# Cutting an output projection in two around other matmuls, and loading the next stage's first inputs early, in a kernel that alternates recurrent attention and gMLP

**Chip, cores, metric.** One core of a Trainium2 chip. The metric is the time of one execution on the device in microseconds (us).

## The reference, cut to what matters

```python
def _A_ref(x, mem0, Wq, Wk, Wv, Wo, seg_len):       # S=2048, D=512, H=32 heads of 128, M=8, seg=32
    mem = mem0
    for s in range(n_seg):                          # 64 segments, one after the other
        h = concat([mem, x[segment s]])             # 8 memory rows + 32 tokens
        q, k, v = h @ Wq, h @ Wk, h @ Wv
        p = softmax(masked(q k^T * scale))
        o = (p v) @ Wo
        mem = o[:, :M]                              # the next segment starts from this
        outs.append(o[:, M:])
def _B_ref(x, w_in, w_sp, b_sp, w_out):             # gMLP
    z = gelu(x @ w_in); z1, z2 = halves(z); z2 = layernorm(z2)
    return (z1 * (w_sp @ z2 + b_sp)) @ w_out
x = x + _A_ref(layernorm(x), ...); x = x + _B_ref(layernorm(x), ...)
x = x + _A_ref(layernorm(x), ...); x = x + _B_ref(layernorm(x), ...)
```

The memory makes attention a chain of 128 segments (64 in each of two blocks). Nothing of segment s+1's memory rows exists before segment s has gone through Wo.

## The kernel before

A segment is one sequence on TensorE. PV is the product of probabilities and values, Wo the output projection; a **change of form** is the switch of TensorE from tiles of one shape (say 128x32) to tiles of another (64x128). The four "fillers" (`fill()`) are matmuls of other work, put where TensorE would wait: projections for the next tile of 128 tokens (`psb`), or an output projection that is not urgent (`pwB`). Of the 64 segments of a block, 45 have `psb` as filler, 12 have `pwB` and 7 have none.

```python
            psS = att.tile([P, 2, 512], F32, name="psS")
            scores(0)                                  # psS: 128x64 tiles; E = exp on ScalarE
            qk_T(3, r3)
            psV = [attO[r].tile([P, 2, 512], F32, name="psV") for r in range(2)]
            v_mm(0, psV[0][:, 0, :])
            fill()                                     # 4 matmuls
            close(0)                                   # mask on VectorE
            nc.vector.tensor_copy(VA[:, 0]..., psV[0][:, 0, :])
            scores(1)
            close(1)
            v_mm(1, psV[1][:, 0, :])
            fill()                                     # 4 matmuls
            nc.scalar.copy(VA[:, 1]..., psV[1][:, 0, :])
            psM = accB.tile([P, 512], F32, name="psM")
            ...                                        # sums for the memory rows: 4 matmuls
            psO = [attO[r].tile([P, 2, 512], F32, name="psO") for r in range(2)]
            pv(0)
            pv(1)                                      # PV of both halves of the heads
            ...                                        # psD: sums for the token rows
            fill()                                     # 8 matmuls
            ...                                        # ScalarE: Rm = 1/psM, Rt = 1/psD by Ln and Exp
            for r in range(2):
                nc.vector.tensor_tensor(out=hview(uT_cur, r, 0, 8), in0=oview(r, 0, 8), in1=...Rm..., op=ALU.mult)
            ...
            spare()                                    # y_add and other work of VectorE
            pw = accB.tile([P, 512], F32, name="pw")
            wo_pass(pw, uT_cur)                        # Wo: 128 weight loads + 128 matmuls
            if s + 1 < NSEG:
                build_hA(s + 1, pw)                    # the next segment's memory rows
            ...
            fill()                                     # 16 matmuls
```

The start of gMLP: w_in whole in two requests, turned row tiles one by one.

```python
        nc.gpsimd.dma_start(w_in_sb[:, :, 0:FH], w_in_v[:, :, FH:FF])
        nc.gpsimd.dma_start(w_in_sb[:, :, FH:FF], w_in_v[:, :, 0:FH])
        ...
        for tt in range(3):
            load_xnT(tt)                               # turning transfer (DMA transpose) of one row tile
        ...
        for tt in range(NT):
            project(tt)
            if tt + 3 < NT:
                load_xnT(tt + 3)
```

The softmax here doesn't subtract the row's maximum and nothing guards it: scores larger than these inputs give would overflow.

## Time and profile before

| | before |
|---|---|
| time, median of 3 runs | 1901.09 us (1898.73 to 1903.06) |
| span of the profiled run | 1906.2 us |
| TensorE busy | 93% |
| segments 0 to 60 of block 0, block 1 | 710.2, 710.5 us |
| segments 61 and 62 together, block 0, block 1 | 33.1, 28.0 us |
| gMLP: projections, block 0, block 1 | 48.2, 47.2 us |
| gMLP: gates and what follows, block 0, block 1 | 125.1, 111.7 us |

The lower part of the table is cut from the trace at the starts of TensorE's groups: a segment begins with its first q matmul (`psm`), the projections with the first `pz`, the gates with the first `pg`; the gates of the last block are counted to TensorE's last matmul. A line of a timeline gives start, duration, engine, source line, operation, output and inputs, and in brackets the idle time just before it with what ended it ("issue": nothing that the profile shows). Durations of matmuls hold latency (a matmul of Wo is recorded with 0.22 us, but 128 of them start within 1.88 us), so what a group costs is the start of the next group minus its own start.

### The profile page before, as it was taken

How to read it: one execution, taken by the hardware profiler on the slowest of the kernel's cores; microseconds unless marked ns; L12 is line 12 of the kernel's file. 1: busy time of each engine (PE TensorE's matmuls, PEld its weight loads, DVE VectorE, ACT ScalarE, POOL GpSimd, SP SyncE). 2: the span in 40 equal slices, each digit the busy share in tenths (PEclk: the TensorE clock that was granted, in tenths of full speed). 3: DMA queues.
4: the chain of work that ended last, by engine and by line, in shares of the span. 5: the costliest groups of instructions: out<-in, count | busy, mean ns of one | idle time of the engine just before them, and what ended most of it. 6: DMA issues, size and time to landing. Idle time of an engine off the chain costs nothing.

```text
span 1906.2 us, 94643 instructions
## 1 busy us (share of the span) xinstructions
PE 1769.2 (93%) x43752; PEld 1020.2 (54%) x43776; DVE 1154.8 (61%) x2700; ACT 1137.9 (60%) x2134; POOL 130.5 (7%) x273
## 2 busy tenths in 40 slices
PE   2999999999999999689989999999999999988898
PEld 1555555555555555335545555555555555544455
DVE  1666666676667766483346666666766676655622
ACT  1666766666666667362136666666766666755511
POOL 5000000000000000022010000000000000002000
PEclk8999999999999999899999999999999999999999
DMA  9100000021002101366640000001200120025554
GB/s 347 43 22 18 18 18 19 22 76 30 18 23 74 29 15 29 97 155 151 141 142 21 21 21 21 21 21 43 79 24 21 51 73 21 15 77 144 115 137 102
DMA packets 165525, 119.93 MB, mean 63 GB/s; under 512 B 112216, under 2 KB 140648, under 8 KB 165128
## 3 DMA queue, kind: packets, MB, share of 16 engines
q1 hardware_dynamic: 143528, 65.11, 13.9%
q0 software_dynamic: 10304, 34.07, 5.7%
q10 hardware_dynamic: 11296, 14.70, 2.6%
q8 instruction: 342, 5.60, 1.2%
q14 instruction: 55, 0.45, 0.1%
HBM read 59.29 MB, written 33.56 MB: 49 GB/s over the span
## 4 chain that ended last, share of the span: by engine, by line
PE 83%; DMA 7%; DVE 4%; issue 3%; ACT 2%; SPq 1%; POOL 0%; DVEq 0%; ACTq 0%; POOLq 0%
PE psm L506 24%; PE psV L506 12%; PE pw L561 12%; PE psb L506 9%; PE pg L306 7%; PE psS L664 5%; PE psO L687 4%; PE pwB L573 3%; PE py L331 2%; PE psD L738 2%; PE pz L245 2%; DMA bsp_bf<-in_B_b_sp_dram 1%; PE psM L728 1%; DMA xs<-xd 1%; DMA xnT<-xb_d 1%
## 5 line engine op out<-in xcount | busy, mean ns | idle before, releaser
L506 PEld LDWEIGHTS <-hA 128*32 128x32 bf16 x12288 | 305.3, 96 | 327.3 <-DVE hA L618 58.9
L643 ACT CAST rows<-psm 128x512 bf16<-128x512 f32 x512 | 299.8, 586 | 203.3 <-PE psm L506 203.3
L561 PE MATMUL pw<-Wo_sb,uT 128*32 128x128 bf16 x16640 | 268.2, 220 | 40.3 <-issue 33.1
L506 PE MATMUL psm<-Wq_sb,hA 128*32 128x512 bf16 x4096 | 279.4, 386 | 22.0 <-DVE hA L618 18.7
L561 PEld LDWEIGHTS <-uT 128*32 128x32 bf16 x16640 | 237.0, 97 | 90.1 <-DVE uT L748 46.1
L506 PE MATMUL psm<-Wk_sb,hA 128*32 128x512 bf16 x4096 | 273.4, 383 | 0.4 <-ACT rowsB L548 0.4
L506 PE MATMUL psV<-Wv_sb,hA 128*32 128x512 bf16 x4096 | 268.0, 382 | 0.0
L647 DVE STREAM_TRANSPOSE QQ<-rows 128x512 bf16<-128x512 bf16 x256 | 182.0, 711 | 90.4 <-ACT rows L643 90.3
L668 ACT ACTIVATE E<-psS 128x448 bf16<-128x448 f32 x256 | 140.0, 547 | 117.8 <-PE psS L664 117.8
L647 DVE STREAM_TRANSPOSE KA<-rows 128x512 bf16<-128x512 bf16 x256 | 181.9, 710 | 40.9 <-ACT rows L643 37.6
L699 DVE TENSOR_TENSOR uT<-psO,Rt 128x384 bf16<-128x384 f32 x256 | 137.9, 539 | 105.4 <-ACT Rt L751 105.4
L748 DVE TENSOR_TENSOR uT<-psO,Rm 128x128 bf16<-128x128 f32 x256 | 62.4, 285 | 180.2 <-PE psD L738 180.2
L306 PE MATMUL pg<-z2n,wspT 128*128 128x344 bf16 x1024 | 161.5, 311 | 0.0
L751 ACT ACTIVATE Rt<-Rt 128x512 f32<-128x512 f32 x256 | 157.4, 629 | 4.1
L611 POOL COPY QQ<-QTB 128x256 bf16<-128x256 bf16 x128 | 51.2, 401 | 1370.3 <-PE psS L664 824.8
L664 PEld LDWEIGHTS <-KA 128*64 128x64 bf16 x2048 | 79.8, 113 | 106.0 <-DVE KA L647 105.2
L746 ACT ACTIVATE Rt<-psD 128x1024 f32<-128x1024 f32 x128 | 131.1, 1024 | 6.1
L506 PEld LDWEIGHTS <-hB 128*32 128x32 bf16 x3072 | 78.4, 96 | 95.7 <-DVE hB L521 26.2
L306 PEld LDWEIGHTS <-wspT 128*128 128x128 bf16 x1024 | 95.7, 98 | 53.0 <-issue 6.8
L671 DVE TENSOR_TENSOR E<-E,maskN 128x448 bf16<-128x448 bf16 x256 | 95.0, 371 | 41.7 <-ACT E L668 41.7
L506 PE MATMUL psb<-Wq_sb,hB 128*32 128x512 bf16 x1024 | 88.6, 385 | 27.3 <-DVE hB L521 27.3
L664 PE MATMUL psS<-QQ,KA 128*64 128x80 bf16 x2048 | 109.9, 208 | 1.1
(127 smaller groups left out, 2300.9 us busy)
## 6 DMA issues: line engine op xcount, KB each, us to landing
Wo_sb<-in_A_Wo_dram POOLq DMA_DIRECT2D x8, 1024.0 KB, 13.5
xs<-xd ACTq DMA_DIRECT2D x32, 256.0 KB
o_d<-o_sb SPq DMA_DIRECT2D x126, 64.0 KB
y_o<-o_d SPq DMA_DIRECT2D x24, 256.0 KB
xd<-y_o SPq DMA_DIRECT2D x22, 256.0 KB
Wq_sb<-in_A_Wq_dram POOLq DMA_DIRECT2D x8, 512.0 KB, 7.3
Wk_sb<-in_A_Wk_dram POOLq DMA_DIRECT2D x8, 512.0 KB, 11.3
Wv_sb<-in_A_Wv_dram POOLq DMA_DIRECT2D x8, 512.0 KB, 11.3
```

The costliest lines, as they stand in the source:

```text
L306: nc.tensor.matmul(pg[t][:, k, 0:344], lhsT=wsp[t][:, st, :], rhs=z2n[:, st, 344 * k:344 * k + 344], start=(st == 0), stop=(st == NT - 1))
L506: nc.tensor.matmul(ps[32 * cg:32 * cg + 32, :], lhsT=lhs(kt, cg), rhs=rhs(kt, cg), start=(kt == 0), stop=(kt == KT - 1), tile_position=(0, ...
L561: nc.tensor.matmul(po[32 * cg:32 * cg + 32, 0:128], lhsT=lhs[:, n, :], rhs=wo_rhs(h, cg), start=(h == 0), stop=(h == H - 1), tile_position ...
L643: nc.scalar.copy(r[:], ps[:])
L647: nc.vector.transpose(out=QQ[:, j % 2, :, 0:32] if j < 2 else KA[:, j % 2], in_=r[:])
L664: nc.tensor.matmul(pS[64 * g:64 * g + 64, i, c0:80 if K is KA else 112], lhsT=K[:, r, n:n + 2, :].rearrange("p h k -> p (h k)"), rhs=q if ...
L668: nc.scalar.activation(out=E[:, r], in_=pS, func=ACT.Exp, scale=scale)
L671: nc.vector.tensor_tensor(out=E[:, r], in0=E[:, r], in1=maskN[:, j4, :].unsqueeze(1).to_broadcast([P, 4, 112]), op=ALU.mult)
L687: nc.tensor.matmul(o if V is VA else ends(o), lhsT=V[64 * g:64 * g + 64, r, i, :], rhs=E[64 * g:64 * g + 64, r, i, c0:c1].rearrange("p (s ...
L699: nc.vector.tensor_tensor(out=hview(uT_nxt, r, 8, 32), in0=oview(r, 8, 32), in1=Rr[:, :, :, 0:24], op=ALU.mult)
L746: nc.scalar.activation(out=Rt[:], in_=psD[:], func=ACT.Ln)
L751: nc.scalar.activation(out=rt, in_=rt, func=ACT.Exp, scale=-1.0)
```

## The change

Its intent: Wo waits for products (`uT`) that wait for the reciprocal of the memory sums, so give TensorE something between. Wo goes in two halves of the heads; the second half's PV and a filler stand between them; the memory sums go per half, so that the first half's come early. For the hand-over to gMLP, w_in comes in four pieces and the first turned row tiles are asked for before attention ends, two row tiles per turning transfer. Three things that go with it are not in the cut: the PSUM buffers of the scores and of the token sums are split by halves, `ln_turn` of the next 128 tokens moves from before Wo to the end of the segment, and the loads of w_sp come two tiles earlier. The diff cut to its core (`...` marks cuts):

```diff
+class _Front:                       # one space: first attention's old buffers, later w_in and turned rows
+    def load_w(self, kt):
+        self.nc.gpsimd.dma_start(self.w_in_sb[:, kt, 0:FH], self.w_in[:, kt, FH:FF])
+        self.nc.gpsimd.dma_start(self.w_in_sb[:, kt, FH:FF], self.w_in[:, kt, 0:FH])
+    def load_rows(self, q):
+        lo = KT * FF + 2 * KT * P * (q % 2)
+        t = self.take(lo, 2 * KT * P).rearrange("p (kt t) -> p kt t", kt=KT)
+        self.nc.sync.dma_start_transpose(out=t, in_=self.xb_d[2 * P * q:2 * P * (q + 1), :]...)
...
-            load_x(t)
+            if t + 2 < NT:
+                load_x(t + 2)                        # residual rows two tiles earlier
...
             scores(1)
             close(1)
-            v_mm(1, psV[1][:, 0, :])
-            fill()
-            nc.scalar.copy(VA[:, 1]..., psV[1][:, 0, :])
-            ...                                      # psM in 4 matmuls
-            pv(0)
-            pv(1)
+            mem_sums(0)                              # 4 small matmuls
+            mem_inverse(0)
+            v_mm(1, psV1[:])
+            nc.scalar.copy(VA[:, 1]..., psV1[:])
+            pv(0)
+            mem_out(0)
+            mem_sums(1)
+            mem_inverse(1)
             ...                                      # psD
             fill()
...
-            wo_pass(pw, uT_cur)
+            wo_pass(pw, uT_cur, range(0, H // 2))
+            pv(1)
+            mem_out(1)
+            fill()
+            ...
+            tok_out(0)
+            wo_pass(pw, uT_cur, range(H // 2, H))
...
             def tail():
+                if tb == NB - 1:                     # the last four segments
+                    front.load_w(j4)
+                    if j4 > 1:
+                        front.load_rows(j4 - 2)
```

## The prediction

> **What bounds the kernel now.** I read the page's first table, then the groups, then the PE timeline of ordinary segments, then the chain and the waits around the two hand-overs from attention to gMLP.
>
> The page's first table, and two groups (busy, mean ns | idle just before, releaser):
>
> ```profile
> PE 1769.2 (93%) x43752; PEld 1020.2 (54%) x43776; DVE 1154.8 (61%) x2700; ACT 1137.9 (60%) x2134; POOL 130.5 (7%) x273
> ...
> L561 PE MATMUL pw<-Wo_sb,uT 128*32 128x128 bf16 x16640 | 268.2, 220 | 40.3 <-issue 33.1
> L561 PEld LDWEIGHTS <-uT 128*32 128x32 bf16 x16640 | 237.0, 97 | 90.1 <-DVE uT L748 46.1
> ```
>
> TensorE is the bound. The trap is the last line: the weight-load row waits 46.1 us for uT before Wo, which is the wait that this change goes after. But the matmul row just above it was idle only 40.3 us before Wo, and 33.1 of that is "issue", not uT: while the weights wait, the filler's matmuls still stream. The PE timeline of one segment (start, duration, group):
>
> ```profile
> 526.02 0.39 PE L506 MATMUL psb<-Wq_sb,hB 128*32 128x512 bf16 x4
> 526.34 0.23 PE L664 MATMUL psS<-QQ,KA 128*64 128x80 bf16 x2
> ...
> 527.91 0.23 PE L728 MATMUL psM<-E,onesG 128*128 128x128 bf16 x1
> ...
> 528.24 0.21 PE L687 MATMUL psO<-E,VA 64*128 64x80 bf16 x2
> ...
> 528.74 0.44 PE L738 MATMUL psD<-E,ones 64*128 64x256 bf16 x8
> 529.11 0.62 PE L506 MATMUL psb<-Wq_sb,hB 128*32 128x512 bf16 x8
> 529.55 1.97 PE L561 MATMUL pw<-Wo_sb,uT 128*32 128x128 bf16 x128
> 531.43 1.05 PE L506 MATMUL psb<-Wk_sb,hB 128*32 128x512 bf16 x16
> ```
>
> Durations contain latency, so I read start to start. The filler psb x8 holds PE 0.44 us (529.11 to 529.55) when Wo follows: both use 128x32 tiles, so 0.22 per four. The filler psb x4 at 526.02 holds it 0.32 when psS follows, in 128x64 tiles. So **a change of tile form costs about 0.10 us** (0.095 at finer resolution; the four psM take 0.33, of which their starts explain 0.23). PV to psD (both 64x128) costs nothing extra. A segment with filler is 11.10 us from first q matmul to the next one if nothing disturbs it, and I find no dependency stall in it. Segments without filler (seven per attention block) take 11.00.
>
> But the segments of the middle of both blocks average about 11.6. The extra is holes like this one inside a group:
>
> ```profile
> 761.38 1.41 PE L561 MATMUL pw<-Wo_sb,uT 128*32 128x128 bf16 x87 [0.36 <-DVE uT L748]
> 766.46 1.33 PE L561 MATMUL pw<-Wo_sb,uT 128*32 128x128 bf16 x41 [3.67 <-issue]
> 773.40 1.90 PE L506 MATMUL psm<-Wq_sb,hA 128*32 128x512 bf16 x16 [5.61 <-DVE hA L618]
> ```
>
> This is the worst (3.67 us); common ones are 0.6 to 1.0 us. They recur at multiples of 256 PE instructions, and the instruction queue of the page has 342 packets of 16 KB: 64 bytes times 256, and 342 times 256 is PE's 87,500 instructions. So PE waits for its program. Wo is 256 instructions in 1.88 us, the densest stretch.
>
> The third line, with the chain around it, shows the hand-over:
>
> ```profile
> 758.29 9.61 DMA o_d<-yB
> 767.91 2.59 DMA y_o<-o_d
> 770.53 0.70 DVE y_o L184
> ```
>
> A store of yB takes 9.6 us because the whole of w_in (1.4 MB) and three turned row tiles were sent at 753; y_add waits for it, and hA stands behind y_add on DVE. Inside gMLP the waits view has this, which delays PE once by 3 us:
>
> ```profile
> DVE xo L340 <- DMA xs<-xd: 31.7, 6, 8.0
> ```
>
> [...] after the 5.61 us wait above, 16 matmuls take 1.68 us start to start, against 0.87 warm.
>
> **The change, part by part.**
>
> 1. *New order on PE.* Before, from psS of half 1: S, V1, filler, M, O0, O1, D, filler, Wo, filler. After: S, M0, V1, O0, M1, D, filler, Wo first half, O1, filler, Wo second half, filler. The four fillers remain, with the same work, but one sits at a later place. Tile forms: S 128x64; V, filler, Wo 128x32; M 128x128; O and D 64x128. In this stretch before: S-V, filler-M, M-O, D-filler, four changes. After: S-M, M-V, V-O, O-M, M-D, D-filler, Wo-O, O-filler, eight. Four more at 0.095 are 0.38 us a segment. The sums per half are eight matmuls of 64 columns for four of 128: about 0.28 us for 0.23, estimated from the 0.035 us pairs of PV; +0.05. PV cut in two: +0.01. Together **+0.44 us**, all on the path, because PE is full there.
>
> 2. *Refill.* A line of 256 instructions that begins with Wo lasts 1.88 us now. After: 128 instructions of Wo in 0.97, 32 of PV in 0.36, 16 of filler in 0.44, 80 of Wo in 0.58, so 2.35 us. A stalled line lasts 2.9 to 3.6 us from its beginning in the trace. The worst hole thus shrinks by about 0.47 us, and averaged over all places where a line's end can fall I get 0.43 going to 0.27: **-0.16 us**. Adding the 8 instructions per segment takes little of it back.
>
> 3. *Sum for attention.* +0.28 us for 114 segments with filler is +32 us. Without filler: the 0.43 wait before Wo goes, but the second half now waits 0.5 for its own product after PV, and there are the drains: +0.2 for 14, +3. Attention: **+35 us**. ScalarE (two Ln of 512 columns for one of 1024, two small Ln and Exp more) and VectorE have 25 to 30% free in a segment and stay out of the way.
>
> 4. *w_in in four pieces over the last four segments, turned rows two segments before the end.* The two segments after seg 60 of each block take 20.27 and 12.81, then 14.50 and 13.47, against 11.00: 17 us lost, counting the half clock. I expect 2 to remain: **-15 us**.
>
> 5. *Two row tiles per turning transfer.* Now a turned tile is asked for when the tile three before is done, and comes up to 5.8 us later (asked 813.9, used 819.7): 1.3 to 1.8 us lost three times per gMLP. With pairs, each is asked two tiles (4.65 us) ahead, so the same loss. The projection takes 48 us where matmuls need 37, but VectorE is busy 39 of the 48 (norms), and the last rows wait for late norms. I book **0**.
>
> 6. *Residual rows loaded two tiles earlier.* The xs waits (3.2 us once, 1.4 twice with slow clock after it) are all in the first gMLP; gone: **-6 us**.
>
> Sum: 1901 + 35 - 15 - 6 = 1915.
>
> **The rivals.** (a) *The wait for uT is real and goes*: 46 us from the weight-load row, so 1901 - 46 - 21 = 1834. For it: that row. Against it: the matmul row's 5.2 us, and the back-to-back starts above. I hardly believe it. (b) *The refill holes vanish altogether*, because the filler in the middle of Wo gives the queue time: 0.43 x 114 = 49 us, against +53 of drains and +0 to 3, minus 21: 1885. For it: Wo is where most holes lie. (c) *A new wait*: the product of half 1 comes only after the second PV, with about 0.5 us of latency against 0.44 us of filler: a tie. VectorE may be held there by y_add. 0.2 us more per segment is 25 us: 1940. (d) *The turned pairs come late*, each wait twice as long, with half clock after it: +8 us, 1923.
>
> **Range and chances.** My sum is 1915. Rival (b) in part is likelier than (c), as the author must have seen some gain, so I say 1909. Attention may be off by 12 us each way, gMLP by 6: 1884 to 1933 holds 8 in 10. Faster by 2% needs 1863, which even (b) does not reach: 0.04. Slower by 2% needs 1939, as in (c): 0.06. The same: 0.90.
>
> **What would show it.** The undisturbed segment grows from 11.10 to about 11.54 us; each of the psM halves, PV halves and both sides of the second PV shows a 0.1 us gap between starts. The weight-load row's wait for uT falls while the time does not. Issue holes before and in Wo fall by about a third. Segments 61 and 62 of each block are near 11.2; xs waits go. The prediction is wrong if drains are hidden (segment under 11.3), if holes vanish, or if Wo's second half waits for uT by more than 0.1 us.

Three of its words stand for measurements. A drain is the 0.10 us that the trace has at a change of form; more than that gap is not shown. The half clock is the granted clock of 0.50 after the wait of 5.61 us (773.40 to 775.08 us) and after one of 3.02 us (903.16 to 906.00). A line of 256 is a packet of the page's instruction queue: 342 of 16 KB before and 346 after, for 87,528 and 88,576 weight loads and matmuls, 256 to each. For the -0.16 us the length of a stalled line is the trace's (segments 2 to 60, from 256 instructions earlier to the end of the stall: 2.4 to 3.6 us, eight in ten 2.8 to 3.4; after, 2.8 to 3.8); the rest of that term is the author's estimate.

## More of the kernel before

TensorE, VectorE and ScalarE run in the order of the text. In the attention block the two engines that issue most DMAs (SyncE, GpSimd) don't: there the framework orders the requests by when it reckons their buffers free.

The profiled run of before took 1908 us by its own clock, 8 us more than the timed median beside the changed kernel (1899.9).

## The result

The changed kernel took 1911.57 us (median of 4 runs, 1910.17 to 1913.9) against 1899.91 for the kernel before, run beside it (4 runs, 1896.72 to 1903.06). The ratio is 1.0063, with a 95% interval of 1.0042 to 1.0083. "The same" by the 2% measure, and slower by 0.6%: 12 us, with 8 to 16 in the interval. The prediction had 8 (1909 for 1901).

The page's first table and the two Wo groups, after:

```profile
PE 1815.1 (95%) x44288; PEld 1044.8 (55%) x44288; DVE 1170.5 (61%) x2700; ACT 1177.4 (62%) x2518; POOL 136.0 (7%) x285
...
L582 PE MATMUL pw<-Wo_sb,uT 128*32 128x128 bf16 x16640 | 285.5, 219 | 19.9 <-issue 10.7
L582 PEld LDWEIGHTS <-uT 128*32 128x32 bf16 x16640 | 244.7, 97 | 90.2 <-DVE uT L745 56.8
```

The weight-load row still waits for uT, now 56.8 us instead of 46.1: that wait was not what the kernel paid for, and it did not go away. What fell is the row above it: idle before Wo from 40.3 to 19.9 us, of that "issue" from 33.1 to 10.7. TensorE is busier (93% to 95%) and not done sooner: the added time is booked as work. The PE timeline of one segment after, from the first half's memory sums to the last filler:

```profile
532.93 0.29 PE L737 MATMUL psM<-E,onesG 128*128 128x64 bf16 x4
533.15 1.05 PE L527 MATMUL psV<-Wv_sb,hA 128*32 128x512 bf16 x16
534.13 0.21 PE L707 MATMUL psO<-E,VA 64*128 64x80 bf16 x2
...
534.70 0.45 PE L774 MATMUL psD<-E,ones 64*128 64x256 bf16 x8
535.08 0.40 PE L527 MATMUL psb<-Wq_sb,hB 128*32 128x512 bf16 x4
535.30 1.07 PE L582 MATMUL pw<-Wo_sb,uT 128*32 128x128 bf16 x64
536.30 0.21 PE L707 MATMUL psO<-E,VA 64*128 64x80 bf16 x2
...
536.64 0.61 PE L527 MATMUL psb<-Wq_sb,hB 128*32 128x512 bf16 x8
537.17 1.08 PE L582 MATMUL pw<-Wo_sb,uT 128*32 128x128 bf16 x64
538.08 1.04 PE L527 MATMUL psb<-Wk_sb,hB 128*32 128x512 bf16 x16
```

Read start to start. psV holds TensorE for 0.98 us (533.15 to 534.13), where it held it for 0.87 before a filler of its own tile form: 0.11 for the change of form. The first half of Wo takes 1.00 (535.30 to 536.30) and the second 0.91: again a change of form. The filler of eight ahead of the second half takes 0.53 (536.64 to 537.17) where eight before Wo took 0.44 before: this 0.08 to 0.09 is a wait for the second half's product, which the timeline of the weight loads names:

```profile
537.17 0.90 PEld L582 LDWEIGHTS <-uT 128*32 128x32 bf16 x64 [0.41 <-DVE uT L745]
```

The shortest segments with filler are now 11.58 us long, before 11.10. Against the groups of a segment of before, the 0.48 are: psV +0.11, the sums +0.11, PV +0.18, psD +0.01, the filler of four -0.09 (its change of form is gone), Wo with the filler behind it +0.08, and +0.08 for the filler ahead of Wo's second half.

Phase by phase from the two traces:

| us | before | after | difference |
|---|---|---|---|
| start | 43.0 | 42.4 | -0.6 |
| segments 0 to 60, both blocks | 1420.6 | 1443.0 | +22.4 |
| segments 61 and 62, both blocks | 61.1 | 45.3 | -15.7 |
| segment 63, Wo, pwB, both blocks | 46.0 | 44.7 | -1.3 |
| gMLP projections, both blocks | 95.4 | 98.5 | +3.1 |
| gMLP gates and next start, both blocks | 236.8 | 232.1 | -4.7 |

I call **hole** what a segment is longer than the shortest segment of its kind (pwB filler, psb filler, none). The mean hole of segments 2 to 60 fell from 0.41 to 0.15 us (mean of the two blocks), and the holes over 0.25 us from 58 to 24 in both blocks.

### The profile page after: what moved, and what is told of

Same layout as the page of the kernel before. It is cut to its first block, busy times and chain, and to the rows that moved or that the text cites. A ratio compares the mean times of both kernels' runs of the same rounds, so it can differ in the third digit from the quotient of the medians.

```text
span 1909.5 us, 96179 instructions
## 1 busy us (share of the span) xinstructions
PE 1815.1 (95%) x44288; PEld 1044.8 (55%) x44288; DVE 1170.5 (61%) x2700; ACT 1177.4 (62%) x2518; POOL 136.0 (7%) x285
## 4 chain that ended last, share of the span: by engine, by line
PE 89%; DVE 4%; DMA 3%; issue 2%; POOL 1%; ACT 1%; DVEq 0%; ACTq 0%; SPq 0%; POOLq 0%
PE psm L527 23%; PE pw L582 13%; PE psV L527 12%; PE psb L527 10%; PE pg L321 8%; PE psS L684 5%; PE psO L707 4%; PE pwB L594 3%; PE psM L737 3%; PE psD L774 2%; PE py L347 2%; PE pz L261 1%; DMA Wo_sb<-in_A_Wo_dram 1%; PE pT L338 1%; DMA Wv_sb<-in_A_Wv_dram 1%
## 5 line engine op out<-in xcount | busy, mean ns | idle before, releaser
L582 PE MATMUL pw<-Wo_sb,uT 128*32 128x128 bf16 x16640 | 285.5, 219 | 19.9 <-issue 10.7
L582 PEld LDWEIGHTS <-uT 128*32 128x32 bf16 x16640 | 244.7, 97 | 90.2 <-DVE uT L745 56.8
L527 PE MATMUL psm<-Wq_sb,hA 128*32 128x512 bf16 x4096 | 272.0, 383 | 10.3 <-DVE hA L638 8.9
L527 PE MATMUL psm<-Wk_sb,hA 128*32 128x512 bf16 x4096 | 268.6, 380 | 0.0
L745 DVE TENSOR_TENSOR uT<-psO,Rm 128x128 bf16<-128x128 f32 x256 | 74.7, 292 | 267.6 <-PE psO L707 263.5
L778 ACT ACTIVATE Rt<-psD 128x512 f32<-128x512 f32 x256 | 136.4, 584 | 0.0
L527 PEld LDWEIGHTS <-hB 128*32 128x32 bf16 x3072 | 73.6, 97 | 83.6 <-DVE hB L542 25.4
L569 ACT CAST rowsB<-psb 128x512 bf16<-128x512 f32 x128 | 74.5, 582 | 56.4 <-PE psb L527 51.0
```

The source lines that it names most:

```text
L527: nc.tensor.matmul(ps[32 * cg:32 * cg + 32, :], lhsT=lhs(kt, cg), rhs=rhs(kt, cg), start=(kt == 0), stop=(kt == KT - 1), tile_position=(0, ...
L582: nc.tensor.matmul(po[32 * cg:32 * cg + 32, 0:128], lhsT=lhs[:, n, :], rhs=wo_rhs(h, cg), start=(h == 0), stop=(h == H - 1), tile_position ...
L778: nc.scalar.activation(out=Rt[:, g, :], in_=psD[g][:], func=ACT.Ln)
```

## The experiments

Twelve kernels ran, each in five rounds against the kernel before, in four sessions. All outputs are right.

**1. The parts apart.** `e1_front_only` has the attention order of before and all the rest of the change; `e2_order_only` has only the new attention order.

```diff
 e1_front_only: the changed kernel, with
-            mem_sums(0) ... wo_pass(pw, uT_cur, range(0, H // 2)); pv(1); fill(); wo_pass(pw, uT_cur, range(H // 2, H))
+            v_mm(1, ...); fill(); psM; pv(0); pv(1); psD; fill(); wo_pass(pw, uT_cur)     # as before
 e2_order_only: the kernel before, with exactly the opposite edit
```

> The attention order of before, with everything else of the change (w_in in pieces, pairs of row tiles per turning transfer, earlier wsp and residual loads). Theory (the terms add): the two segments after number 60 of each block fall from 33.1 and 28.0 us to about 22, gMLP's gate phase loses its residual-row waits, the projection gains 2 us twice: about 19 us less than before, near 1881, and the undisturbed segment stays 11.10 us. Rival (the hand-over gain was luck of the profiled run, which was 8 us longer than the timed ones): only 10 us less, near 1890.

> The new attention order alone, gMLP and its loads as before. Theory (eight changes of tile form instead of four, shorter program waits): 22 to 32 us more than before, 1922 to 1932, undisturbed segment 11.58 us. Rival (the new order is neutral on the clock and the loss of the whole lies in gMLP): 1900. The slow hand-over of before (33.1 and 28.0 us for two segments) should be back.

Measured, against 1903.81 us for before in that session: `e1_front_only` 1891.04 us, ratio 0.9926 (0.9907 to 0.9944); `e2_order_only` 1937.96 us, ratio 1.0172 (1.0150 to 1.0194). So the new order costs about 33 us (22 to 32 expected, with the expected shortest segment of 11.58 us), and the rest gives back about 14. For `e1_front_only` the number is the rival's (1890, expected if the slow hand-over was luck of one profiled run), but the trace is the theory's: the hand-over does fall as expected. The theory missed mainly because it booked a gain of 4 us on the projections. The product of the two ratios is 1.0097; the changed kernel has 1.0063, some 6 us better. In the trace of `e2_order_only` segments 61 and 62 are worse than before (34.2 and 31.4 us in the two blocks), which is 4.5 us of that. In the trace of `e1_front_only` segments 61 and 62 fall to 22.5 and 23.4 us, and the gates by 4.4, but the projections grow by 4.0.

**2. Pairs of row tiles undone.** On `e1_front_only`, one row tile per turning transfer, in four slots, so tile t + 4 is asked for after tile t (three tiles lie between, as the expectation counts it) and as soon as its slot is free:

```diff
-        lo = KT * FF + 2 * KT * P * (q % 2)
-        ...dma_start_transpose(out=t, in_=self.xb_d[2 * P * q:2 * P * (q + 1), :]...)
+        lo = KT * FF + KT * P * (q % 4)
+        ...dma_start_transpose(out=t, in_=self.xb_d[P * q:P * (q + 1), :]...)
...
+            if tt + 4 < NT:
+                front.load_rows(tt + 4)
```

> As e1, but one row tile per turning transfer in four slots, so that each is asked for three tiles ahead instead of two. Theory (a turned pair asked two tiles ahead comes late by about 1.6 us three times per projection): the projection falls from 49 to about 45 us, 4 to 8 us less than e1 in all. Rival (VectorE's norms and the last rows' late norms bound the projection, transfers are hidden anyway): the same as e1 within 2 us.

Measured 1886.31 us, ratio 0.9899 (0.9881 to 0.9918). The same program ran three times more (experiment 6), and the mean of its four ratios is 0.9909, so by the times alone the gain over `e1_front_only` is 0.2%, no more than the scatter. The phase itself is a little clearer: both projections together take 98.3 to 99.9 us in four of the five kernels with pairs (98.5 in the changed kernel, 99.4 in `e1_front_only`, 98.3 in `e4_pv_joined`, 99.9 in `e8_after_shift`) and 94.6 to 96.4 in the seven runs with single tiles. The fifth with pairs, `e9_sums_whole`, takes 95.1, though TensorE idles as long there as in the changed kernel (17.6 and 17.9 us): its last two tiles run at full clock (granted clock 1.00, 4.65 us), where those of the changed kernel get 0.63 and 0.71 (7.3 and 6.5 us). So the phase moves by some 3 us with whether a lower clock follows the last wait, and that the longer projections come from the pairs is likely but not shown. The view of `pz` has what ended the idle time before it, first of the changed kernel, then of `e3_single_tiles`:

```profile
  DMA front<-xb_d: 14.8, 6
  ACT z L264: 3.1, 4
```

```profile
  ACT z L264: 9.5, 6
  DMA front<-xb_d: 7.9, 2
```

Both lines are TensorE's: us, and how often. Six waits for turned rows (14.8 us) became two (7.9), while TensorE waits more often for ScalarE to free `pz` (9.5 for 3.1), so that only part is gained. The two that remain are one in each gMLP, for the last tiles, whose normalised rows are themselves late (in block 0 they are stored from 835.35 us on, and the transfers go out at 837.39). One sees them in the changed kernel too, with a lower clock behind (granted 0.63, 24 matmuls in 7.49 us; elsewhere 4.81, at 1.00):

```profile
842.14 4.81 PE L261 MATMUL pz<-front 128*128 128x512 bf16 x24 [0.68 <-ACT z L264]
852.27 7.49 PE L261 MATMUL pz<-front 128*128 128x512 bf16 x24 [5.32 <-DMA front<-xb_d]
```

This is the best version found: by the mean of its four ratios 0.9% faster than before, and 1.5% faster than the changed kernel.

**3. The second PV joined to the first stretch.** On the changed kernel, `pv(1)` goes right after psD, so two changes of form fall away and only a filler of eight stands between the halves of Wo (not in the cut: psM and the second half of V exchange their PSUM buffers):

```diff
             ...                                      # psD
+            pv(1)
             fill()
+            mem_out(1)
...
             wo_pass(pw, uT_cur, range(0, H // 2))
-            pv(1)
-            mem_out(1)
             fill()
```

> The changed kernel with the second PV moved back from between the Wo halves to straight after the sums of tokens, where it has the same tile form; two changes of form fewer, Wo still in halves with the filler between, memory sums still per half. Theory (a change of form costs 0.095 us of PE each): undisturbed segment 11.39 us instead of 11.58, 20 us less than the changed kernel, near 1891, less up to 6 us if the program waits grow because Wo's halves are now closer. Rival (the second PV between the halves gives the program queue the time it needs): program waits go back to those of before and the time stays near 1905 to 1911. Rival (drains are hidden): segment stays 11.58.

Measured 1902.94 us, ratio 0.9991 (0.9975 to 1.0006). The shortest segment falls from 11.58 to 11.26 us: psD 0.38 to 0.29 and the first half of Wo 1.00 to 0.89 (the two changes of form, 0.20), the filler of eight 0.53 to 0.43 (the wait for the product). Three of the same lines of `e4_pv_joined`:

```profile
543.92 1.07 PE L582 MATMUL pw<-Wo_sb,uT 128*32 128x128 bf16 x64
544.82 0.60 PE L527 MATMUL psb<-Wq_sb,hB 128*32 128x512 bf16 x8
545.25 1.07 PE L582 MATMUL pw<-Wo_sb,uT 128*32 128x128 bf16 x64
```

But the holes grew from 0.15 to 0.35 us per segment. Of the 0.32 us gained in work, 0.20 went back into holes, which leaves 0.12 x 114 = 14 us; by the ratios it is 14 (0.9991 against 1.0063). (The two traces give 10.5 us for segments 0 to 60: with `pwB` filler the shortest segment fell by 0.10 only.) What came back is not all TensorE's program. Of the idle stretches over 0.15 us in segments 2 to 60 of both blocks, those without a releaser went from 7.2 to 19.0 us, but 7.6 us are new waits for ScalarE to empty `psb`, up to 1.44 us at once, of which the changed kernel has none. So PV between the halves costs changes of form and saves waits for the program and for ScalarE; about half of what came back is shown to be the program's.

**4. Where the holes come from.** `e5_shift` is `e3_single_tiles`, `e8_after_shift` the changed kernel, each with 128 more TensorE instructions once at the very start, half of a line of 256:

```diff
+        if first:
+            dmy = accB.tile([P, 512], F32, name="dmy")
+            for k in range(64):
+                nc.tensor.matmul(dmy[:, 0:128], lhsT=ones[:], rhs=ones[:], start=True, stop=True, ...)
         ln_turn(0)
```

> Built on e3: 64 extra 128x128 matmuls (128 TensorE instructions) once at the very start, with an output nobody reads; every later instruction moves by half of a 256-instruction line. Theory (the holes inside segments are waits for TensorE's program, one per line, and cost where a line's end falls together with dense small matmuls): the single holes move to other segments and groups, their sum in each block stays within 4 us of e3's (27 and 24 us), and the time is that of e3 within 0.3% (ratio .987 to .993). Rival (the holes are waits for data or for another engine): they stay in the same segments, within a segment of where they were. Third possibility: e3 has a lucky place of its lines; then the sum moves by over 6 us and the ratio by over 0.4%.

> The changed kernel with the same 128 extra instructions at the start. Theory (the new order needs less queue time than the old one wherever the lines end): holes stay near 0.15 us per segment (before 0.41), time that of the changed kernel within 0.3% (ratio 1.003 to 1.009 over before). Rival (the small holes of the changed kernel are luck of where its lines end): holes go up to 0.3 per segment and the time by 15 us (ratio 1.014).

Lengths of seven segments of block 0 (56 and 52 have pwB filler, at least 11.43; the others at least 11.10), from the starts of their first matmuls:

| segment | 52 | 53 | 54 | 55 | 56 | 57 | 58 |
|---|---|---|---|---|---|---|---|
| before | 11.43 | 11.78 | 11.10 | 12.18 | 11.43 | 11.48 | 11.10 |
| e3_single_tiles | 11.43 | 11.74 | 11.10 | 11.90 | 11.47 | 12.34 | 11.10 |
| e5_shift | 12.44 | 11.10 | 12.08 | 11.10 | 12.15 | 11.10 | 11.35 |

The PE timeline has two of them as breaks within Wo, in `e3_single_tiles`:

```profile
671.60 0.34 PE L582 MATMUL pw<-Wo_sb,uT 128*32 128x128 bf16 x9 [0.45 <-issue]
694.27 0.68 PE L582 MATMUL pw<-Wo_sb,uT 128*32 128x128 bf16 x33 [0.62 <-issue]
```

These are in segments 53 and 55. In `e5_shift` the corresponding ones are in segments 52 and 54:

```profile
662.02 0.34 PE L582 MATMUL pw<-Wo_sb,uT 128*32 128x128 bf16 x9 [0.78 <-issue]
685.21 0.51 PE L582 MATMUL pw<-Wo_sb,uT 128*32 128x128 bf16 x21 [0.80 <-issue]
```

The holes jumped to the segments that had been whole, at the same data and the same work. The table shows where it is clearest: of the 62 holes over 0.25 us of `e3_single_tiles` in both blocks, 31 shrank to under 0.1, and 20 segments still have one over 0.25. The count of instructions settles it. Number TensorE's instructions in each trace in order of time (weight loads, matmuls and its semaphore instructions). In segments 2 to 60 of both blocks TensorE has 54 idle stretches over 0.15 us without a releaser in the kernel before (28.5 us), 16 in the changed kernel (7.2 us), 54 in `e3_single_tiles` (29.8) and 56 in `e5_shift` (36.2). Every one of them stands at the same place of its 256: the number modulo 256 is 194, and in three of the four traces it drops once, for all that follow, by 1 (before: by 13), presumably where records are missing; in the changed kernel it is 194 throughout. And in the traces of before and after each of them (54 and 16) ends 1.2 to 1.6 us after a packet of 16 KB of the instruction queue has landed: TensorE waited for its program. Of the stretches with a named releaser (in before 6.0 us for `hA`, 2.2 for `uT`, 0.4 for a copy of ScalarE) none stands there; those are waits for data, also counted in what I call holes.

The sum of the holes over segments 2 to 60 was 28.3 and 30.1 us in the two blocks, in `e3_single_tiles` 27.2 and 23.6 (23.5 to 24.6 in block 1 in its three repeats, experiment 6). In block 1 that is 6.4 us more, where I had allowed 4 and set over 6, with a ratio over 0.4% off, as the sign of a lucky place. The ratio did not move so far, but where the lines end does matter a little. The time was 1889.13 us, ratio 0.9927 (0.9906 to 0.9948), against 0.9899 to 0.9917 for the unshifted program. `e8_after_shift` took 1911.84 us, ratio 1.0049 (1.0031 to 1.0067), with a mean hole of 0.15 us, the same as without the shift. So the small holes of the new order are no luck of where its lines end.

**5. The memory sums whole again.** On the changed kernel, all four matmuls of the memory sums after the first PV:

```diff
-            mem_sums(0)
-            mem_inverse(0)
             v_mm(1, psV1[:])
             nc.scalar.copy(VA[:, 1]..., psV1[:])
             pv(0)
-            mem_out(0)
-            mem_sums(1)
-            mem_inverse(1)
+            ...                                      # psM as before: 4 matmuls, one Ln, one Exp
+            mem_out(0)
```

> The changed kernel with the memory sums not halved: all four matmuls of them after the first PV. Theory A (the halving only costs: one more change of tile form and eight small matmuls for four, as the prediction counted it): segment 11.58 to 11.43, about 18 us faster than the changed kernel, ratio .997. Theory B (the halves buy time for the first uT: from the sums' end the Ln of 0.38, the Exp of 0.42 and the product of 0.25 us take 1.25 us, and only psD and one filler of four stand between, 0.6 us): the first half of Wo waits 0.5 us for uT in each segment, segment about 11.95; some of it is given back by fewer program holes, so time +30 over the changed kernel, ratio about 1.022.

Measured 1985.66 us, ratio 1.0443 (1.0420 to 1.0465), some 72 us slower than the changed kernel, more than twice what the second theory expected. The PE timeline of a segment of `e9_sums_whole`:

```profile
372.29 0.40 PE L527 MATMUL psb<-Wq_sb,hB 128*32 128x512 bf16 x4
373.23 1.08 PE L582 MATMUL pw<-Wo_sb,uT 128*32 128x128 bf16 x64 [0.54 <-DVE uT L734]
```

The filler of four holds TensorE for 0.94 us instead of 0.23: Wo's first half waits 0.7 us for its product even in the shortest segments. The shortest segment is 12.11 us (11.95 expected). The holes did not shrink in exchange: 0.21 us on average, for 0.15. Here the wait for uT is real, and it shows on the matmul row of the page, not only on the weight-load row:

```profile
L582 PE MATMUL pw<-Wo_sb,uT 128*32 128x128 bf16 x16640 | 283.7, 220 | 95.6 <-DVE uT L734 80.6
L582 PEld LDWEIGHTS <-uT 128*32 128x32 bf16 x16640 | 235.9, 97 | 177.8 <-DVE uT L734 159.6
```

Without the halves of the sums, then, the new order costs another 0.53 us a segment. The prediction counted them only as a cost.

**6. The hand-over: three edits that changed nothing.** On `e3_single_tiles`, I moved the requests for w_in and for the turned rows in the text:

```diff
 e7_w_whole:      -  front.load_w(j4)
                  +  if j4 == 0:
                  +      for k in range(4): front.load_w(k)
 e10_rows_early:  -  if j4 > 1:
                  -      for k in range(2): front.load_rows(2 * (j4 - 2) + k)
                  +  for k in {0: (0, 1, 2), 3: (3,)}.get(j4, ()): front.load_rows(k)
 e11_both_early:  both
```

> Built on e3: all four pieces of w_in are asked for at the end of segment 60, the turned row tiles stay where e3 has them. Theory A (the volume of w_in, 1.4 MB in one go, delayed the store of yB and the reads behind it): segments 61 and 62 go back from 22.5 us towards 33 in block 0 and 28 in block 1, time +10 to +15 over e3, ratio about .997. Theory B (the turning transfers that stood in front of that store in SyncE's queue delayed it): segments 61 and 62 stay under 24 us and the time is e3's, ratio .988 to .992.

> Built on e3: w_in stays in pieces over the last four segments, but the first three turned row tiles are asked for at the end of segment 60, as the kernel before did. Theory B (the turning transfers in SyncE's queue ahead of the store of yB, 1.2 to 2.6 us each on the queue, hold that store and the reads behind it): segments 61 and 62 go back towards 33 us in block 0 and 28 in block 1 from 22.6 and 22.8; time +10 to +15 over e3, ratio about .997. Rival (it takes both, the volume of w_in and the turning transfers at once): segments 61 and 62 stay under 25 us, ratio .988 to .993.

> As e10_rows_early, and all of w_in asked for at the end of segment 60 too: the arrangement of the kernel before. Both theories expect 33 and 28 us for segments 61 and 62 (ratio about .997); it tells whether the volume adds anything to what the turning transfers do alone: theory B says nothing above 2 us, the rival says all of it. If this one stays under 25 us too, the cause lies in neither and is where the kernel before allocates the tiles or issues the requests.

Measured 1886.06, 1890.38 and 1889.07 us, ratios 0.9911 (0.9890 to 0.9931), 0.9917 (0.9900 to 0.9933) and 0.9910 (0.9895 to 0.9925); segments 61 and 62 stayed at 22.4 to 23.3 us. A comparison of the instruction streams showed that on all five engines the three kernels are `e3_single_tiles`, instruction for instruction in the same order: the framework had put the requests where their buffers come free. In `e7_w_whole` and in `e3_single_tiles` alike the pieces of w_in start at 701, 707, 739.5 to 740.3 and 753.7 to 754.5 us. The three say nothing of the cause. They do measure how well one program repeats: 0.9899, 0.9910, 0.9911, 0.9917. A difference of 0.2% between two kernels means nothing here.

**7. The hand-over again, moved by the buffers.** A request can be held back by what its buffer must wait for. In `e12_rows_last`, the first two turned row tiles lie where segment 60's product reads last; in `e13_w_whole_last`, w_in comes in two whole requests that overlap what that product reads.

```diff
 e12_rows_last:    -  lo = KT * FF + KT * P * (q % 4)
                   +  lo = KT * P * (q % 4)                       # w_in moves up by 4 * KT * P
                   -  wo_last(G, range(8 * q, 8 * q + 8), pwB)
                   +  wo_last(G, range(8 * (3 - q), 8 * (3 - q) + 8), pwB)
 e13_w_whole_last: -  dma_start(self.w_in_sb[:, kt, 0:FH], self.w_in[:, kt, FH:FF])    # and the other half
                   +  if kt == 0: dma_start(self.w_in_sb[:, :, 0:FH], self.w_in[:, :, FH:FF])    # and the other half
```

> e7, e10 and e11 turned out to be e3's program instruction for instruction on the DMA queues (the framework orders SyncE and GpSimd by when the buffers are free, not by the place in the text), so they tested nothing of the hand-over. Here the buffers do it: on e3, the first two turned row tiles lie where segment 60's product reads last, so the turning transfers can only start after it, ahead of the store of yB; the pieces of w_in come earlier still. In the kernel before that store was issued 3.4 us later than in e3 (758.3, after two turning transfers) and landed 9.6 us after its issue instead of 4.1. Theory 1 (queue order): segment 61 of block 0 grows by about 3.4 us or more, to 14 or more. Theory 2 (volume alone): stays at 11.2 to 11.4. Time over e3 +0 to +7 us, ratio .990 to .994.

> On e3, w_in in two whole requests as in the kernel before, which can only start after segment 60's product; the turned row tiles stay early as in e3. Theory 2 (volume): the store of yB takes about 5.5 us longer to land, segment 61 of block 0 grows to 15 to 17 us, block 1 less; time +5 to +10, ratio .993 to .996. Theory 1 (queue order alone): segments 61 and 62 stay at 11.2 to 11.4, ratio .990.

Measured: `e12_rows_last` 1889.62 us, ratio 0.9918 (0.9904 to 0.9931); `e13_w_whole_last` 1892.80 us, ratio 0.9935 (0.9923 to 0.9948). This time the traces show the requests where they were meant to be: the turning transfers of `e12_rows_last` ahead of the store of yB in the lines below, and w_in of `e13_w_whole_last` on GpSimd's queue at 756.83 and 757.58 us (before: 753.76 and 754.51; in `e12_rows_last` its last piece at 740.7). SyncE's queue at the end of segment 60 of block 0 (start, duration), first before, then `e3_single_tiles`, `e12_rows_last` and `e13_w_whole_last`:

```profile
753.51 4.69 SPq L231 DMA_TRANSPOSE xnT<-xb_d  x2
758.29 0.56 SPq L567 DMA_DIRECT2D o_d<-yB  x1
...
767.91 0.35 SPq L179 DMA_DIRECT2D y_o<-o_d  x1
771.25 0.32 SPq L185 DMA_DIRECT2D xd<-y_o  x1
```

```profile
754.76 0.56 SPq L588 DMA_DIRECT2D o_d<-yB  x1
759.05 0.35 SPq L204 DMA_DIRECT2D y_o<-o_d  x1
762.95 0.32 SPq L210 DMA_DIRECT2D xd<-y_o  x1
```

```profile
754.04 1.19 SPq L160 DMA_TRANSPOSE front<-xb_d  x1
...
755.92 2.12 SPq L160 DMA_TRANSPOSE front<-xb_d  x1
758.14 0.56 SPq L588 DMA_DIRECT2D o_d<-yB  x1
760.97 0.35 SPq L204 DMA_DIRECT2D y_o<-o_d  x1
764.58 0.32 SPq L210 DMA_DIRECT2D xd<-y_o  x1
```

```profile
757.66 0.56 SPq L589 DMA_DIRECT2D o_d<-yB  x1
764.15 0.35 SPq L205 DMA_DIRECT2D y_o<-o_d  x1
767.43 0.32 SPq L211 DMA_DIRECT2D xd<-y_o  x1
```

Count from the start of segment 61 (753.13, 753.93, 754.37 and 756.84 us). The store of yB goes out after 5.2, 0.8, 3.8 and 0.8 us: the turning transfers ahead of it on the queue cost 2.9 to 4.3 (one held it 1.2 us by the median of before's 32, 3.0 at most). From the store's issue to the read behind it there are 9.6, 4.3, 2.8 and 6.5 us: the whole of w_in at once costs 2.2 without the turning transfers and 6.8 with them. The last line of each fence is issued when y_add is done: after 18.1, 9.0, 10.2 and 10.6 us. Segment 61 is 20.27, 11.38, 12.37 and 12.74 us long. What exceeds 9.0 us comes out one for one in the segment's length over 11.18 us, its neighbour in `e3_single_tiles`: 9.1, 0.2, 1.2 and 1.6. So the hand-over has a deadline; either cause alone misses it by 1.2 to 1.6 us, and both together, as before, by 9. That is block 0; segments 61 and 62 of both blocks together take 45.4, 48.5, 49.9 and 61.1 us (`e3_single_tiles`, `e12_rows_last`, `e13_w_whole_last`, before), so in the sum too the single causes cost 3 and 5 us and both together 16. Both theories had expected more of the single causes (14 us or more, 15 to 17), since in the kernel before the two had only been seen together. A lower clock can also follow a wait: in segment 62 of `e12_rows_last` and of before, behind waits of 2.15 and 5.61 us, the q and k groups took 5.25 and 5.22 us instead of 3.58, at a granted clock of 0.67 and 0.68 (in before 0.50 over the first 1.68 us). The length of the wait alone does not decide it: behind 2.45 us in `e13_w_whole_last` the segment kept its 11.17 us.

## Why the prediction was right, step by step

The time was predicted as 1909 us in a range of 1884 to 1933, with 0.90 for "the same". It came out at 1911.57 and "the same". The mechanism, changes of form against program waits, holds, but two terms were off by enough to be worth naming, and they partly cancelled, which is luck. By the traces alone the parts sum to +3 us and not to 12, because the profiled run of before was itself 8 us longer than the timed median; so the parts are known to a few us only.

1. **New order on PE, +0.44 us a segment.** Measured +0.48 (11.10 to 11.58). The changes of form and the halved sums came to 0.39 to 0.40 instead of 0.44; a change of form costs 0.09 to 0.11 us. The rest, +0.08, is the wait for the second product. In the prediction's words: "0.5 us of latency against 0.44 us of filler: a tie". It was no tie: the filler held 0.53. Rival (c) was thus true to a little under half of its 0.2 us. That this is a wait is shown by `e4_pv_joined`, where the product comes earlier and the filler holds 0.43.
2. **Refill, -0.16 us.** This is the step that was mis-sized: holes went from 0.41 to 0.15, by -0.26. The prediction reckoned with the worst place of a line's end within Wo; the trace has fewer stalls rather than shorter ones (54 of 0.53 us on average became 16 of 0.45); presumably the sums, PV and fillers along the whole stretch gave the queue more. `e4_pv_joined` shows the direction (program stalls of 19.0 us for 7.2 with PV moved out of Wo), `e8_after_shift` that it was not luck. Which of the interruptions gave how much stays open. Rival (b), that all holes vanish, did not happen, and would not have paid for the new order anyway (0.41 us of holes against 0.48).
3. **Attention, +35 us.** 0.48 - 0.26 = 0.22 us for 114 segments is +25, and the trace has +22.4 for segments 0 to 60. By the timed runs of `e2_order_only` the order costs +33, with 4.5 of it in segments 61 and 62. So +35 was too high, by 2 to 13 us according to which of these one takes. The prediction's closing shading from 1915 to 1909 took this for likely; the result of 1911.57 lies between the two and does not decide.
4. **Hand-over, -15 us.** Measured -15.7. Its cause was put down to w_in and the turned rows together ("because the whole of w_in (1.4 MB) and three turned row tiles were sent at 753"); experiment 7 shows that it did take both. (Of the three turned row tiles two went out ahead of the store; the third stands behind it, at 758.91.) The credit for moving them is to the buffers, not to the place of the calls in the text.
5. **Pairs of row tiles, 0.** Off by +3.1 us: the projections grew from 95.4 to 98.5 us. TensorE's waits for turned rows did stay nearly the same, as the step said (13.8 us before, 14.8 after); its waits for ScalarE to free `pz` grew from 1.3 to 3.1. With single tiles asked for four tiles ahead the projections take 94.6 to 96.4. Rival (d), +8, had the direction, and its lower clock is there (granted 0.63 and 0.71); but `e9_sums_whole`, also with pairs, takes 95.1 without it (experiment 2), so the 3.1 are not shown to be the pairs' alone.
6. **Residual rows earlier, -6 us.** Measured -4.7 in the gates; the waits view after has no wait of VectorE's `xo` for `xs` any more, before it had 31.7 us in six.
7. **What would show it.** The prediction expected the weight-load row's wait for uT to fall. It rose from 46.1 to 56.8 us, and still was nearly free, because the matmul row's was 7.7. It also expected the "issue" holes before and in Wo to fall by about a third; on Wo's matmul row they fell by two thirds (33.1 to 10.7), which is step 2 again. `e9_sums_whole`, with 80.6 on the matmul row, shows what a wait looks like that is paid.

Rival (a), 1834 us, is out: the uT wait of the kernel before was hidden by the matmuls already streaming.

## What to carry to other kernels

Before putting work of another shape between two dependent matmul groups, count the changes of tile form (0.1 us each here) and look whether the wait stands on the matmul row or only on the weight-load row: only the former was paid here. Where TensorE has gaps with no releaser that move when instructions are added, count its instructions between them and look when the packets of the instruction queue land: here the gaps recurred every 256 and ended 1.2 to 1.6 us after a packet, so TensorE waited for its program, and work of a less dense kind placed there was partly free: 0.26 of 0.48 us came back. When an edit moves a request and nothing changes, compare the instruction streams first: a framework that orders queues itself may have built the same program.
